# Queues of a fused DeltaNet and mixer kernel, searched anew up to the second token group

## The chip, the cores and the metric

The kernel runs on one core of a Trainium2 chip. The metric is the device time of one execution in microseconds: the median over the runs, 591.4 us here, from 591.33 to 591.42 over three runs. Two versions that differ by less than about 0.2% can hardly be told apart by it.

## The reference

Two blocks follow each other. The first is a delta-rule attention over 4 batches, 8 heads, 768 tokens and a head width of 48, written as a recurrence over tokens:

```python
k_n = k / (np.linalg.norm(k, axis=-1, keepdims=True) + 1e-06)
for t in range(S):
    y[:, :, t] = q_t @ state
    v_old = state^T k_t
    state = state + beta_t * outer(k_t, v_t - v_old)
```

The second mixes its output x (4 x 768 x 384): a low-rank mix over tokens and a channel block.

```python
h = xt @ U @ V                       # rank 32, over the 768 tokens
u = x + h.transpose(0, 2, 1)
ch = np.maximum(u @ w_ch1, 0.0) @ w_ch2      # 384 -> 1536 -> 384
return u + ch
```

The weights U, V, w_ch1 and w_ch2 come as float64 and are turned into float32 on the core.

## The kernel before

**Units.** The attention is cut into 8 units of work, one for each half (384 tokens, six chunks of 64) of each batch; units 0 and 1 make up batch 0. A unit loads k, q and v, turns k and q on PE (L668 or L405, copied out by ACT at L682), forms the k-by-k products (L704; diagonal blocks taken out by ACT at L714 and DVE at L717, the rest copied by ACT at L725, for units 0 and 1 spread by L729) and the q-by-k products (masked by DVE at L736). It norms the keys (`norms`: L611 on ACT, L614 to L619 on DVE, the rows for v at L625 and L628). Then it solves the triangular systems (`blocks`): DVE transposes the diagonals (L781), does fifteen pairs of small multiply and subtract steps (L790, L796), transposes back (L803) and the halves are joined on PE, ACT and DVE (L812 to L926: PE L847, L861, L887/890, L905/908; ACT L852, L895, L914, L926; DVE L865). Two slots of SBUF hold the units in turn, so unit 2 can be loaded when the recurrence is through unit 0.

**Recurrence.** `recur` walks the twelve chunks of a batch: PE L1107, L1135, L972, L986, with DVE at L1120 and L1147 and ACT's L956 that writes the rows of x. For units 0 and 1 `prepare` (PE L1011 and L1022, ACT L1030 and L1035) folds the triangular solution into k and v first.

**Weights.** Fourteen slices are loaded in float64 halves (L1221: slice 0 is U, 1 is V, then six of w_ch1, six of w_ch2) into three buffers in turn, and DVE converts each with five instructions (L1244, L1250, L1256, L1262, L1272), with ACT's L1229 in between. A slice's load waits until its buffer's last slice is through L1262. L1179 forms sums of the second matrix's slices.

**Token groups.** Each batch has three groups of 256 tokens. `front` of a group mixes tokens (PE L1469, DVE L1476, PE L1486, DVE L1495) and turns the result (PE L405 or L1514, ACT L1517). `wide` runs the channel block: PE L1580, ACT L1545, sums on DVE (L1607), PE L1695, and DVE adds the products to X (L1620), which SP writes out.

**Order.** Nothing is scheduled at run time. Every part of the work is a coroutine that yields operations, and for each engine a written list, `ORDER`, says whose operation comes next. An entry is the name of a part: its ordinal, and behind dots that of the parts it started. `11.4` is the fifth part that part 11 started. The function `run` walks the five lists and emits an instruction as soon as it is at the head of its engine's list; the instructions of an engine then run strictly in the list's order, and a list of DMA issues on SP or POOL is such a queue too. Planned costs (`cost`, `lat`, the constants `SPAN, PHASE = 3.413, 2.0` of the array's clock) are used when the lists are searched and to emit in a sensible order; they change no instruction.

The names that the change and the prediction use:

- 0, 1: loads of k, unit 0; 2, 3: beta of the first and second halves (PE L579, ACT L587, DVE L595); 4: the recurrence of batch 0, with 4.0 to 4.3 its `prepare` steps.
- 8: norms of unit 0; 9 and 10: its k and q products; 11: its `blocks`, with 11.2 and 11.4 the joins of the two halves of its chunks and 11.1 and 11.3 the copies of the diagonals; 12 to 17: its loads of q, v and z (two parts each, one on SP and one on POOL; z is a second copy of some of k).
- 18 to 29: the same for unit 1 (18 norms, 19 and 20 products, 21 `blocks`, 22, 23 k; 24, 25 q; 26, 27 v; 28, 29 z). 30 to 37: unit 2 (33 `blocks`; 34 k, 35 q, 36 v, 37 z, a part for both queues each). 38 to 45: unit 3.
- 78: weights: 78.0 to 78.13 load slices 0 to 13, 78.14 to 78.27 convert them, 78.26.1 and 78.27.1 form sums.
- 81, 82, 83: `front` of groups 0, 1, 2 of batch 0; 98, 99, 100: their `wide`.

Of the kernel before, what the change touches and what calls it, by code (L numbers as in the profile page):

```python
# [26 lines left out]
def kernel(  # L27
# [100 lines left out]
    def advance(i, value, at):  # L128
# [28 lines left out]
        5.4 99.1*2 5.5 40.0.0.0 5 83 99.2*2 99.3*2 99.4 48.0 99.4 41.2*2 47.0 99.7 47.1 47.0.0.0 47.1.0.0  # L157
        41.4*2 99.5*2 48.1 41.2 41.4*2 41.2 99.7 99.8 48.1.0.0 5 99.8 5.6 5 48.0.0.0 5 99.9 5 99.9 5.7 5*2
        99.9 5 5.6 99.9 5.8 5.7 5 99.10 5*2 100.0 5.9 5 100.0 5.8 5 100.0 5 100.0 5.9 5 5.10 5 100.1 5.11 5
        5.10 100.1 5 5.11 100.1*2 84 100.2*2 100.3*2 100.4*2 100.5 100.7 100.5 49.2*2 55.0.0.0 84 55.1.0.0  # L160
        100.7 100.8 49.2 49.4*2 49.2 100.8 84 100.9*2 6 85 100.9 6 100.9 56.0.0.0 56.1.0.0 6 100.10 49.4*2
        6.0 6 101.0*2 85 6.1 6 101.1*2 6 101.1 6 101.1 6.2 6 101.2*2 6.1 6 101.2*2 6 6.3 6.2 101.3 6 101.3 6
        6.4 6.3 6 101.4 6 101.4 6.5 6 101.4 6 101.4 6.4 6 6.5 101.5*2 101.7*2 57.2*2 57.4*2 86 57.4*2 57.2*2
# [1613 lines left out]
```

## Time and profile before

| | before |
|---|---|
| median of three runs | 591.4 us |
| lowest, highest | 591.33, 591.42 us |
| the profiled execution | 589.15 us |
| its span, first to last instruction | 587.4 us |
| PE busy | 545.3 us (93%) |
| PE weight loads busy | 491.1 us (84%) |
| DVE busy | 456.2 us (78%) |
| ACT busy | 227.3 us (39%) |
| POOL busy | 118.1 us (20%) |
| granted PE clock, mean | 0.939 |

The profile is one execution. Its time, 589.15 us, is the span and 1.75 us around it, and lies 2.25 us under the median of the runs. Rows give the start from the first instruction, the busy time of a group of equal instructions, the engine, the line of the kernel, and in brackets the idle time of the engine ahead of it with what ended it. "SPq" and "POOLq" are the queues that issue DMAs. PEclk is the share of the full clock that the array was granted. A wait for several semaphores is put down to one of them.

### The profile page before, as it was taken

To read this page: it belongs to the slowest core of one execution; us is meant where nothing else is said; L and a number is where in the kernel's file an instruction comes from. 1 tells how busy PE (TensorE), PEld (TensorE's weight loads), DVE (VectorE), ACT (ScalarE), POOL (GpSimd) and SP (SyncE) were. 2 spreads that over 40 slices of the span, in tenths; PEclk is the share of its full clock that TensorE was granted. 3 is DMA by queue.
4 is the path that set the end of the run, shared out by engine and by line. 5 is a ranking of instruction groups with operands and counts; after the bars stand their busy time and mean duration, and the time that the engine had idled before them with its cause. 6 is when DMAs were issued, how large, how long until landed. Compare 5 with 4: busy or idle time off the path is not lost.

```text
span 587.4 us, 25542 instructions
## 1 busy us (share of the span) xinstructions
PE 545.3 (93%) x11460; PEld 491.1 (84%) x11460; DVE 456.2 (78%) x1086; ACT 227.3 (39%) x483; POOL 118.1 (20%) x205
## 2 busy tenths in 40 slices
PE   5697778799999999999999999999999999999997
PEld 4586677588888987997897798988889999999997
DVE  6898999999899898899878888888547574555552
ACT  4447476544433623344344305324423422131220
POOL 8132050311205304340252253301000000000000
PEclk9576666799999999999999999999999999999999
DMA  9634676652104314223212433200000000000013
GB/s 157 85 76 128 192 188 166 134 91 63 29 4 83 68 22 83 74 53 63 48 30 61 80 75 71 60 29 3 2 5 1 2 1 1 1 2 1 1 42 119
DMA packets 79213, 35.17 MB, mean 60 GB/s; under 512 B 65600, under 2 KB 76992, under 8 KB 79104
## 3 DMA queue, kind: packets, MB, share of 16 engines
q1 hardware_dynamic: 71200, 24.10, 18.9%
q0 software_dynamic: 6304, 9.15, 7.2%
q8 instruction: 90, 1.47, 1.0%
q10 hardware_dynamic: 1600, 0.30, 0.3%
q14 instruction: 19, 0.16, 0.1%
HBM read 28.80 MB, written 4.72 MB: 57 GB/s over the span
## 4 chain that ended last, share of the span: by engine, by line
PE 79%; DVE 7%; ACT 5%; DMA 4%; issue 3%; SPq 1%; POOL 1%; DVEq 0%; ACTq 0%; POOLq 0%
PE P L1695 24%; PE P L1580 12%; PE P L1430 12%; PE P L393 10%; PE P L704 3%; DMA wide<-in_moe_w_ch_dram 2%; PE P L668 2%; PE P L1066 2%; PE P L1090 1%; PE P L972 1%; PE P L1486 1%; PE P L986 1%; PE P L1135 1%; PE P L1514 1%; PE P L861 1%
## 5 line engine op out<-in xcount | busy, mean ns | idle before, releaser
L1695 PE MATMUL P<-w_sb,hs 128*128 128x192 f32 x480 | 84.2, 329 | 0.1
L1580 PE MATMUL P<-ut,w_sb 128*128 128x256 f32 x348 | 81.8, 386 | 0.1
L1695 PEld LDWEIGHTS P<-w_sb,hs 128*128 128x128 f32 x480 | 77.7, 190 | 1.3 <-issue 0.3
L1580 PEld LDWEIGHTS P<-ut,w_sb 128*128 128x128 f32 x348 | 64.1, 190 | 9.4 <-issue 0.6
L796 DVE TENSOR_TENSOR xt<-xt,prod 128x112 f32<-128x112 f32 (+21 forms) x200 | 64.6, 323 | 6.9
L790 DVE TENSOR_TENSOR prod<-gs,xt 128x112 f32<-128x112 f32 (+21 forms) x200 | 63.7, 319 | 3.9
L1620 DVE TENSOR_TENSOR X<-X,P 128x192 f32<-128x192 f32 x86 | 29.6, 349 | 36.1 <-PE P L1695 34.2
L1545 ACT ACTIVATE hs<-P 128x512 f32<-128x512 f32 x42 | 24.8, 597 | 62.1 <-PE P L1580 51.0
L393 PE MATMUL P<-ut,w_sb 64*64 64x256 f32 x624 | 43.0, 384 | 1.2 <-ACT hs L1545 0.9
L956 ACT COPY X<-P 64x192 f32<-64x192 f32 x96 | 30.0, 312 | 28.8 <-PE P L986 27.2
L704 PE MATMUL P<-slot 48*64 48x64 f32 x1536 | 33.5, 245 | 1.9 <-ACT slot L682 1.6
L704 PEld LDWEIGHTS P<-slot 48*64 48x64 f32 x1536 | 30.0, 157 | 6.1 <-ACT slot L682 2.5
L933 POOL MEMSET slot<- 32x384 f32 x32 | 13.4, 420 | 102.6 <-PE P L890 40.4
L1412 DVE TENSOR_TENSOR hs<-hs,P 128x512 f32<-128x512 f32 x30 | 20.1, 684 | 17.5 <-PE P L1430 9.2
L1695 PE MATMUL P<-w_sb,S 128*128 128x192 f32 x192 | 33.7, 330 | 0.0
L926 ACT COPY slot<-zz 32x384 f32<-32x384 f32 x64 | 32.3, 508 | 1.0
L1099 ACT COPY z<-P 128x192 f32<-128x192 f32 x36 | 11.5, 319 | 53.3 <-PE P L1090 46.4
L1695 PEld LDWEIGHTS P<-w_sb,S 128*128 128x128 f32 x192 | 31.1, 190 | 0.6 <-DVE xt L796 0.3
L548 POOL DMA_DIRECT2D slot<-in_k_dram x44 | 28.7, 657 | 12.3 <-PE P L1135 10.6
L668 PE MATMUL P<-ident,slot 128*128 128x128 f32 x108 | 20.0, 343 | 11.3 <-DMA slot<-in_k_dram 5.7
L1430 PE MATMUL P<-slot 128*128 128x128 f32 x240 | 29.7, 276 | 0.0
L1695 PE MATMUL P<-w_sb,slot 128*128 128x192 f32 x168 | 29.1, 327 | 0.0
(171 smaller groups left out, 1140.9 us busy)
## 6 DMA issues: line engine op xcount, KB each, us to landing
out_dram<-X SPq DMA_DIRECT2D x22, 192.0 KB, 2.0
X<-in_moe_w_ch_dram SPq DMA_DIRECT2D x10, 384.0 KB, 4.4
wide<-in_moe_w_ch_dram SPq DMA_DIRECT2D x10, 384.0 KB, 4.4
slot<-in_k_dram SPq DMA_DIRECT2D x48, 72.0 KB, 3.7
slot<-in_k_dram POOLq DMA_DIRECT2D x44, 72.0 KB, 3.1
slot<-in_v_dram SPq DMA_DIRECT2D x32, 72.0 KB, 3.7
slot<-in_v_dram POOLq DMA_DIRECT2D x32, 72.0 KB, 3.2
hs<-in_moe_w_ch_dram SPq DMA_DIRECT2D x4, 384.0 KB, 5.7
```

Source lines behind the costliest of these rows:

```text
L393: nc.tensor.matmul(to[half(g)], w[half(r), half(g)], x[half(r)], start=start, stop=stop, skip_group_check=True,)
L548: queue.dma_start(out=t[half(1 - g if name == "z" else g), :, to, 0:D], in_=src[b, 4 * g + s, hf * UC * L : (hf + 1) * UC * L, :].rearrang ...
L668: nc.tensor.transpose(p_t[:, c // 3, c % 3], t[:, c, 2 * j : 2 * j + 2].rearrange("p s d -> p (s d)"), ident,)
L704: nc.tensor.matmul(p_g[half(g ^ (par * i)), par, c], kq[rows, c, j, 0, half(g)], kq[rows, c, j, i, half(g)], start=True, stop=True,)
L790: nc.vector.tensor_tensor(out=prod, in0=gb[:, :, j : j + 1, j + 1 :].to_broadcast([128, split, m, w]), in1=xb[:, :, 0:m, j : j + 1].to_bro ...
L796: nc.vector.tensor_tensor(out=xb[:, :, 0:m, j + 1 :], in0=xb[:, :, 0:m, j + 1 :], in1=prod, op=ALU.subtract,)
L926: nc.scalar.copy(pg[quarter(i), :, at, :, a : a + BK], cut(zc, h)[quarter(i)].rearrange("p r (c j) t -> p r c j t", j=2),)
L956: nc.scalar.copy(x[half(c % 2), c // 2, 4 * D * g : 4 * D * (g + 1)].rearrange("p (j r d) -> p r j d", r=2, d=D), states(p_y)[half(g)],)
L1430: nc.tensor.matmul(bank[:, q], w_block(w)[:, q // 2, 128 * (q % 2) : 128 * (q % 2) + 128], token(b, i, t), start=c == 0 and q == 0, stop=True,
L1580: nc.tensor.matmul(p_f[:, x], w(x, t), ut[:, t], start=(t == 0), stop=(t == KT - 1))
L1620: nc.vector.tensor_tensor(out=to, in0=to, in1=p, op=ALU.add)
L1695: nc.tensor.matmul(to, of[0], of[1], start=of[2], stop=of[3], skip_group_check=True)
```

## The change

The same steps stand in the same five lists, in another order from the start up to a point in the `wide` of group 0 (98.7 on PE, and the same place on the other engines); from there on the lists are equal but for one entry (79) that issues nothing. No step is added, taken away or computed in another form. One line of the lists is saved, so lines behind L178 move up by one in the changed kernel; this text uses the numbers of the kernel before.

What is moved, engine by engine:

- PE: the beta matmuls of the second half (`3`) before unit 1's second k turn (19.1) and not around its products; the joins 11.2 and 11.4 of unit 0 closer together; the joins of unit 1 (21.2, 21.4) later among the first steps of the recurrence; in `wide` of group 0 the first product (98.0) ahead of group 1's mix (82), and all of 98.2 ahead of unit 2's join 33.2.
- DVE: U's last conversion before unit 0's norms; V's conversion (78.15) earlier; the transpose back of unit 1 (L803) ahead of the two masks 20.1.0.0; two small steps of unit 2 (30, 32.0.0.0) ahead of slice 12's conversion (78.26); the sums 78.26.1 ahead of unit 2's last steps (33).
- ACT: the warm-up of the square root table (`1`) first; the copies of the diagonals and L729 of unit 1 in another order; relu of 98.0 behind the copies for group 1 and unit 3.
- POOL: beta (`2`) ahead of the first loads; loads of q and z in another order.
- SP: three of the four pieces of V (78.1) behind k and q of unit 1, the last one between the v loads of unit 0 (14); v of unit 1 (26) partly ahead of the last of 14; one more load of unit 2 ahead of the second half of slice 9 (78.9); loads of unit 3 in another order.

The lists, cut to the part that differs most:

```diff
     ORDER = dict(
         pe="""
-        9.0 9.1 9.0.0.0 9.1.0.0 2*2 19.0 19.1 3 19.0.0.0 3 19.1.0.0 10.0 10.1 10.0.0.0 20.0 11.4 10.1.0.0
-        11.4 11.2*2 11.4*2 11.2*2 20.1 11.4*4 20.0.0.0 11.2*4 20.1.0.0 4.1 4.0*2 4.1 21.2*2 4 4.4 21.2 4
-        21.2 4.5 4 21.4*2 21.2 4 4.5 4.6 4*2 21.2 4.6 21.2*2 4.7 4*2 4.8 4.7 4 21.4 4.9 4 21.4 4 4.9 4.8
-        4.2*2 21.4*2 4 4.10 21.4*2 4*2 4.10 4.11 4*2 4.11 4.3 32.0 31.0 4.3 31.1 4.12 4 31.0.0.0 31.1.0.0 4
-        4.12 32.1 4.13 4*2 4.13 4.14 4 4.15 4 4.14 4.15 79 32.0.0.0 81 32.1.0.0 81*2 40.0 82 98.0*2 39.0
-        39.1 82 98.1 40.1 39.1.0.0 39.0.0.0 98.1 98.2 33.2*2 98.2 98.3*2 98.4 33.4*2 33.2 98.4 33.2 98.5
-        33.4*2 33.2*2 98.5 98.7 83 33.2 33.4 33.2 33.4 98.7 33.4*2 98.8 5 5.0 5 40.1.0.0 5 98.8 5.1 5 98.9 5
-        98.9 5 5.1 98.9 5 98.9 5.2 5 98.10 5 5.2 5.3 5 99.0 5 99.0 5 5.3 5.4 5 99.0 5 99.0 5.5 5 99.1*2 5
...
+        9.0 9.1 9.0.0.0 9.1.0.0 2*2 19.0 3*2 19.1 19.0.0.0 19.1.0.0 10.0 10.1 10.0.0.0 20.0 11.4*2 11.2*2
+        11.4*2 10.1.0.0 11.2*2 20.1 11.4*4 20.0.0.0 11.2*4 20.1.0.0 4.0 4.1 4.0 4.1 4 21.2*2 4.4 4 21.2*2
+        4.5 21.4 4 21.4 4 21.2*2 4.5 4.6 4*2 4.7 21.2*2 4.6 4*2 4.7 4.8 4 21.4 4.9 4 21.4 4 4.9 4.8 4.2*2
+        21.4*2 4 4.10 4 21.4*2 4 4.11 4.10 4*2 4.3 4.11 32.0 31.0 4.3 31.1 4.12 4 31.0.0.0 31.1.0.0 4 4.12
+        32.1 4.13 4*2 4.13 4.14 4 4.15 4 4.14 4.15 32.0.0.0 79 81 32.1.0.0 81*2 40.0 98.0 82 98.0 39.0 82
+        98.1 39.1 40.1 39.1.0.0 39.0.0.0 98.1 98.2*2 33.2*2 98.3*2 98.4 33.2*2 33.4*2 98.4 98.5 33.2 33.4*2
+        33.2 98.5 98.7 33.2*2 83 33.4*2 98.7 33.4*2 98.8 5 5.0 5 40.1.0.0 5 98.8 5.1 5 98.9 5 98.9 5 5.1
+        98.9 5 98.9 5.2 5 98.10 5 5.2 5.3 5 99.0 5 99.0 5 5.3 5.4 5 99.0 5 99.0 5.5 5 99.1*2 5 5.4 99.1*2
...
         dve="""
-        9.0.0 9.1.0 78.14*3 9.0.0.0*2 9.1.0.0*2 78.14 11 2 8 11*12 8 11 19.0.0.0*2 11*4 19.1.0.0*2 11.4 21
-        78.14 3 10.0.0.0 11.2 18 78.15 21 78.15 10.1.0.0 10.0.0.0 21 18 21 11.4*2 10.1.0.0 11.4 21*3 11.2*3
-        8 21 78.15 21*7 20.0.0.0*2 21*2 20.1.0.0 21 20.1.0.0 78.15*2 21.2 21.4 18 78.16 4 78.16*4 4 78.17*2
-        4 21.2*3 78.17*3 4 78.18*2 4 78.18*3 4 78.19*2 4 78.19 4 78.19 4 78.19 78.20*2 4 78.20 21.4 4
-        78.20*2 21.4 78.21 21.4 78.21*4 4 78.22*2 4 78.22*2 4 78.22 4 78.23*2 4 78.23*3 78.24*5 4 78.25*2
-        31.0.0.0*2 31.1.0.0*2 4 33 4 30 4 78.25 4 33*2 4 78.25*2 33*2 78.26 32.0.0.0 78.26 81 33 78.26 81
-        32.1.0.0*2 78.26 33 78.26 33 82 33*2 32.0.0.0 30 33*8 33.4 33.2 78.26.1*3 39.0.0.0 78.27 98.2.1*3
-        39.1.0.0 78.26.1 39.0.0.0 30 78.27*4 39.1.0.0 33.2*3 33.4*2 78.27.1 33.4 41 98.5.1*2 78.27.1*2
-        98.7.0 98.5.1 78.27.1 38 83 41 98.6 5 98.7.1 41*3 38 98.8.0 5 98.8.1 41*3 5 41 5 41*2 40.1.0.0
...
+        9.0.0 9.1.0 78.14*3 9.0.0.0*2 78.14 9.1.0.0*2 11 2 78.14 8 11*10 8 19.0.0.0*2 11*7 11.4 19.1.0.0*2
+        11.2 21 3 78.15 18 78.15 21*3 10.0.0.0 21 10.0.0.0 11.4 10.1.0.0 21 11.4*2 11.2 21*2 11.2*2 18 78.15
+        10.1.0.0 21 8 21*4 20.0.0.0*2 21*5 20.1.0.0*2 78.15 21.2 78.15 18 78.16*2 4 78.16*3 4 21.4 78.17*2
+        21.2 78.17 4 21.2*2 78.17*2 4 78.18*2 4 78.18*3 4 78.19*2 4 78.19 4 78.19 4 78.19 78.20*2 4 78.20
+        21.4 4 78.20*2 21.4 78.21*2 21.4 78.21*3 4 78.22*2 4 78.22*2 4 78.22 4 78.23*2 4 78.23*3 78.24*5 4
+        78.25*2 31.0.0.0*2 31.1.0.0*2 4 33 4 30 4 78.25 4 33*2 4 78.25*2 33*2 30 32.0.0.0 78.26*2 81 78.26
+        32.1.0.0 81 32.1.0.0 33*5 78.26 82 32.0.0.0 78.26 78.26.1*3 33*8 33.2 30 39.0.0.0 78.27 39.0.0.0
+        78.27 78.26.1 39.1.0.0 33.4 78.27*3 33.2*3 98.2.1 78.27.1*2 33.4*2 39.1.0.0 33.4 41 78.27.1 98.7.0
+        98.2.1 98.5.1*2 78.27.1 98.5.1 98.2.1 38 83 41 98.6 5 98.7.1 41*3 38 98.8.0 5 98.8.1 41*3 5 41 5
...
         act="""
-        1*4 9.0.0 1 9.1.0 9.0.0.0 9.1.0.0 78.14.0 2*2 9.0.0.0*2 8 19.0.0 9.0.0.0 9.1.0.0*3 19.0.0.0 19.1.0
-        19.0.0.0 19.1.0.0 10.0.0 10.1.0 3*2 20.0.0 19.1.0.0 18 11.4.0 11.4 11.4.0 19.0.0.0 19.1.0.0 11.2
-        11.2.0*2 11.4 11.3 11.4 11.1*3 11.4 11.3 11.1 11.3*2 11.2 19.1.0.0 19.0.0.0 20.1.0 78.15.0 11.2*2
-        4.0*2 4.1 21.2 21.2.0*2 78.16.0 4.4 4.1 4.4 78.17.0 21.4.0*2 4.5 21.4 78.18.0 4.5 21.2*2 4.6 78.19.0
-        4.6 21.2 4.7 21.1*2 4.7 21.1*2 78.20.0 4.9*2 4.8*2 78.21.0 4.2*2 21.3 21.4 21.3 21.4 78.22.0 21.3
-        21.4 21.3 78.23.0 4.10 4.11*2 32.0.0 4.10 78.24.0 31.0.0 4.3*2 31.1.0 31.0.0.0 31.1.0.0 4.12*2
-        31.1.0.0 30 31.0.0.0 4.13*2 78.25.0 4.14*2 4.15*2 32.1.0 78.26.0 81 40.0.0 98.0.0 82 39.1.0 39.0.0
-        39.0.0.0 40.1.0 98.1.0 33.2 98.2.0 78.27.0 39.1.0.0 39.0.0.0 33.4 98.3.0 39.1.0.0 33.1*2 98.4.0
-        98.5.0 33.2 33.1*2 33.4 33.2 38 33.2 33.4*2 5 33.3 5.0*2 5 33.3*3 98.9 5.1*2 5*2 99.0 5.2*2 5.3 5
...
+        1*5 9.0.0 9.1.0 9.0.0.0 78.14.0 9.1.0.0 2*2 9.0.0.0 9.1.0.0 8 9.1.0.0*2 9.0.0.0*2 19.0.0 19.0.0.0
+        19.1.0 3*2 19.1.0.0 19.0.0.0 10.0.0 10.1.0 20.0.0 11.4 11.4.0*2 11.2.0 18 19.1.0.0 19.0.0.0 11.2
+        11.2.0 11.4 11.3 11.4 11.1*4 11.4 19.0.0.0 11.3*3 11.2 20.1.0 11.2*2 19.1.0.0*2 78.15.0 4.0*2 21.2.0
+        4.1 21.2.0 4.1 78.16.0 21.2 21.4.0 4.4*2 78.17.0 21.1 21.4 21.4.0 4.5 78.18.0 4.5 21.1 21.2 4.6
+        21.2*2 78.19.0 4.6 21.1 4.7 21.1 4.7 78.20.0 4.9 4.8*2 4.9 78.21.0 4.2*2 21.3 21.4 21.3*2 78.22.0
+        21.4*2 4.10 21.3 78.23.0 4.11*2 4.10 32.0.0 78.24.0 31.0.0 4.3*2 31.1.0 31.0.0.0 31.1.0.0 4.12*2
+        31.1.0.0 30 31.0.0.0 4.13*2 78.25.0 4.14 4.15*2 4.14 32.1.0 81 40.0.0 78.26.0 82 39.0.0 39.1.0
+        39.1.0.0 40.1.0 98.0.0 39.0.0.0 98.1.0 33.2 98.2.0 39.0.0.0 78.27.0 33.4 98.3.0 98.4.0 33.2 98.5.0
+        39.1.0.0 33.2*2 38 33.4 33.1*4 33.4*2 5 33.3 5.0*2 5 33.3*3 98.9 5.1*2 5*2 99.0 5.2*2 5.3 5 5.3
...
         pool="""
-        11.0 13 23 78.0 2*3 17 23 25 23 13 23 25 13*2 25 29 25 21.0 15*2 29 17 15*2 11.3 11.1 11.3 11.1 27*4
-        21.1*2 34*3 35 31.0 35 33.0 21.3*2 35 34 35 43*2 42*4 43 39.0 43 36*2 37 41.0 36 44 36 33.1 37 33.1
-        44*2 33.3 44 33.3 45 51*2 50*4 45 47.0 49.0 51*2 53 41.1*2 52*2 41.3 52*2 53 41.3 110*8 61 55.0 59*6
...
+        2 11.0 2 78.0 2 23*2 13*2 25 23*2 13*2 17 25 21.0 15*2 29 15*2 17 29 25*2 11.3 11.1 27*2 11.1 27
+        11.3 27 21.1*2 34*3 35 31.0 35 21.3*2 35*2 34 33.0 43*3 42*2 36*2 42 36 42 37 39.0 36 43 37 41.0
+        33.1*2 44*2 33.3*2 44*2 45 51*2 50*4 47.0 49.0 51 45 51 53 41.1*2 52*2 41.3 52*2 53 41.3 110*8 61
...
         sp="""
-        0*4 78.1 22*2 12*2 22*2 78.1*2 12 78.1 12 24*3 14*4 24 16 26*4 78.2*2 28 16 78.3*2 78.4*2 28 78.5*2
-        78.6*2 78.7*2 78.8*2 78.9 35 34*4 35*2 78.9 35 78.10*2 78.11*2 36*3 37 36 78.12*2 43*4 37 42*3 45 42
-        44*2 78.13*2 44 45 44 51*4 50*4 52*2 53 52*2 53 110*2 59 110*6 61 59 99.9.1 59*3 61 58*2 59*2
...
+        0*4 22 78.1 22 12 22 24*2 22 16 24*2 12*3 78.1*2 28 14*2 78.1 14 26 14 78.2 16 26*2 78.2 26 78.3*2
+        78.4*2 78.5*2 78.6*2 28 78.7*2 78.8*2 78.9 34 35*2 34*3 35*2 78.9 78.10*2 78.11*2 36*2 37*2 36
+        78.12*2 36 43*4 42*4 44*2 45 78.13*2 44*2 45 51*4 50*4 52*2 53 52*2 53 110*2 59 110*6 61 59 99.9.1
...
```

More of the change, by code (lines that the diff above doesn't have):

```diff
@@ L159 @@
[L159 to L163, printed above, removed]
@@ new lines @@
+        99.9.1 49 99.10.0 5 49 5 49*2 5 49 5 49*2 5 49 5 49*9 46 49*2 84 49 100.2.1*2 49.2 49.4 55.1.0
+        55.0.0 100.5.1*2 100.2.1 100.5.1 100.7.0 84 55.1.0.0 55.0.0.0 55.1.0.0 100.7.1 55.0.0.0 100.6 57
+        100.8.0 54 100.8.1 56.0.0 57*4 56.1.0 6 85 100.9.0 56.0.0.0 56.1.0.0 56.0.0.0 6 57 56.1.0.0 100.9.1
+        100.10.0 57*7 6 57 6 57*2 6 57*2 6 57*3 101.2.1 57 6 57 6 57*2 6 57 6 57*5 6 54 57*3 57.2 101.2.1
+        101.7.0 57.4 101.2.1 101.5.1*3 101.7.1 54 86 101.6 101.8.0 101.8.1 63.0.0 64.0.0 101.9.0 101.9.1
@@ new lines @@
+        63.1.0 63.0.0.0 6 63.0.0.0 101.10.1 101.10.0 64.1.0 63.1.0.0*2 65 62 65*2 6 65 64.0.0.0 62 6
+        64.0.0.0 65*2 6 65*2 6 65*3 6 65 6 102.2.1 65 6 65 6 65*3 6 102.2.1*2 65 6 65 102.5.1*2 65 62 87 65
+        102.5.1 102.7.0 65*3 102.7.1 65 102.8.0 65 102.6 102.8.1 87 65 102.9.0 65 71.0.0 65 102.9.1 102.10.0
+        64.1.0.0*2 71.1.0 65*4 71.1.0.0 65 71.0.0.0 65.4 71.0.0.0 71.1.0.0 65.2 73 72.1.0 72.0.0 70 73*2
+        72.1.0.0 103.2.1 73 72.1.0.0 73*3 103.2.1*2 73 103.7.0 103.5.1*2 72.0.0.0 73 7 103.5.1 103.7.1 73
@@ new lines @@
+        94.1.2 94.2.2 105.1*2 105.3.1 105.3.0 95.0 94.1.3 95.0*4 94.5.0 94.2.3 95.0 105.4.0 94.0 105.2
+        94.4.1 95.0 105.4.1 94.1.4 105.5.0 95.0*2 106.1*2 106.0 91 95.0 106.1 105.6.0 106.0 105.5.1 106.3.0
+        95.1.1 96.0*3 95.2.1 106.0 95.0 95.1.2 95.4.1 106.3.1 106.2 96.0 95.3.1 95.1.3 106.4.0 95.2.2 96.0
+        106.4.1 96.0*3 95.5.0 106.5.0 96.0*2 95.1.4 95.2.3 92 96.1.1 96.2.1 107.0 96.1.2 96.2.2 106.6.0
+        107.1*2 106.5.1 96.2.3 97.0*4 107.1 107.0*2 107.3.0 97.0*2 107.3.1 96.3.1 97.0*3 107.4.0 96.0 96.1.3
@@ L262 @@
+        59*3 61 58*2 59*2 99.10.0 58*2 98.10.0 98.9.1 59 100.9.1 60*4 111*8 67*5 69 100.10.0 67*3 68*3
+        101.10.1 68 112*2 75 112*6 101.9.1 75*2 77*2 75*3 66 75*2 66 102.9.1 74 66 74 69 66 102.10.0 74*2
+        76*4 103.9.1 103.10.0 108.6.0 105.5.1 107.5.1 107.6.0 106.5.1 104.10.1 109.3.1 108.5.1 104.9.1
+        106.6.0 105.6.0 109.5.0 109.5.1 109.6.0
         """,
```

89 lines of the change are left out of this document (37 added, 52 removed).

## The prediction

> **What bounds the kernel now.** I read the page's slices first, then the busy time by stretch, then what the engines wait for.
>
> ```profile
> PE   5697778799999999999999999999999999999997
> DVE  6898999999899898899878888888547574555552
> PEclk9576666799999999999999999999999999999999
> ```
>
> A slice is 587.4/40 = 14.7 us. PE is full and its clock high from the ninth slice on; in the eight slices before, PE has holes, a clock of about a half, and DVE is the full one. The busy time by stretch (columns: length, then busy time and count of PE, PEld, DVE, ACT, POOL; then PE's clock, DMA share, GB/s) says the same in numbers:
>
> ```profile
> 10.00:59.00 49.00, 36.62 (x1126) 33.46 (x1120) 44.10 (x118) 28.59 (x56) 13.92 (x23) 0.65 0.56 106
> 59.00:94.00 35.00, 25.73 (x890) 23.49 (x892) 33.66 (x58) 19.69 (x39) 8.59 (x14) 0.64 0.71 184
> 94.00:118.80 24.80, 20.09 (x592) 16.57 (x588) 23.01 (x48) 14.58 (x27) 6.97 (x12) 0.75 0.67 148
> 155.00:587.40 432.40, 422.58 (x7883) 382.92 (x7881) 316.36 (x772) 144.00 (x326) 71.25 (x121) 1.00 0.17 37
> ```
>
> Up to 118.8 DVE is the bound (44.10 + 33.66 + 23.01 = 100.8 of 108.8 us busy from 10 on); from there PE is (422.58 of 432.40 us behind 155). The switch is the first matmul on finished attention rows: the turn of `front` for group 0, L405, which waits for DVE's L1495. DVE's own waits, in order of time, and that turn:
>
> ```profile
> 10.73 0.26 DVE L1244 TENSOR_SCALAR power<-X 128x192 int32<-128x192 int32 x1 [1.42 <-DMA X<-in_moe_U_dram]
> 24.56 0.74 DVE L717 SCALAR_TENSOR_TENSOR slot<-P,even,slot 128x192 f32<-128x192 f32 x2 [0.23 <-ACT slot L714]
> 52.10 0.56 DVE L736 TENSOR_TENSOR slot<-P,mask_u 128x384 f32<-128x384 f32 x1 [0.94 <-ACT slot L914]
> 93.66 0.56 DVE L1244 TENSOR_SCALAR power<-wide 128x768 int32<-128x768 int32 x1 [0.40 <-DMA wide<-in_moe_w_ch_dram]
> 114.67 0.72 DVE L1244 TENSOR_SCALAR power<-X 128x768 int32<-128x768 int32 x1 [0.64 <-DMA X<-in_moe_w_ch_dram]
> 118.83 0.93 PE L405 MATMUL P<-ident,X 64*64 64x64 f32 x48 [1.31 <-DVE X L1495]
> ```
>
> The steps are the same before and after, and the queues are the same behind group 0's `wide`. So the change is worth (a) what it moves L405, plus (b) what PE waits more or less between L405 and that point. I go through both in order of time.
>
> **Start, to 33 us.** The load of U stays the third transfer on POOL's queue, but two beta transfers (48 KB) stand ahead of it in place of a q and a k piece (72 KB): DVE's 1.42 us wait for it can shrink by 0 to 1.4. The pieces ahead are little smaller, and behind the wait ACT's L714 comes soon; I take 0.3.
>
> ```profile
> 14.91 0.26 DVE L595 STREAM_TRANSPOSE betas<-beta_rows 128x128 f32<-128x128 f32 x1
> 15.30 0.18 DVE L614 TENSOR_SCALAR norm<-norm 128x32 f32<-128x32 f32 x1
> ```
>
> U's last conversion, L1272, moves from behind unit 1's L781 to between L595 and L614, where DVE has 15.30 - 15.17 = 0.13 free: 0.1 gained, and neither less than 0 nor more than that gap. The 0.23 wait on L714 of unit 1 should go, because unit 1's k arrives earlier:
>
> ```profile
> 10.00:15.00 5.00, 3.73 (x128) 3.33 (x122) 4.24 (x10) 3.12 (x7) 3.73 (x6) 0.90 1.17 172
> 20.13 1.51 PE L668 MATMUL P<-ident,slot 128*128 128x128 f32 x6 [4.89 <-issue]
> 26.76 2.82 PE L668 MATMUL P<-ident,slot 128*128 128x128 f32 x12
> 29.18 3.43 SPq L548 DMA_DIRECT2D slot<-in_v_dram  x4
> ```
>
> PE stands for 4.89 us before unit 1's second k turn. No releaser is named; I read it as the last k pieces, since three of the four V pieces (192 KB) are issued ahead of them. After, three V pieces leave the front and about two q pieces (72 KB) enter: 0.43 MB at 172 GB/s is 2.5 us. The batch-1 beta matmuls (L579, `3`) fill part of the gap. So unit 0's q turns (26.76 to 29.58) end near 26.2. DVE does not go faster for that, but L717, now three steps earlier, finds its data. Start: 0.3 + 0.1 + 0.2 = 0.6 gained.
>
> **The 0.94 wait at 52.**
>
> ```profile
> 48.55 1.12 ACT L729 ACTIVATE hs<-slot,even 128x384 f32<-128x384 f32 x2
> 50.26 0.94 ACT L1229 ACTIVATE power<-power,bias_e 128x768 int32<-128x768 int32 x1
> 51.09 0.97 ACT L914 ACTIVATE slot<-P 32x384 f32<-32x384 f32 x2
> 52.57 2.05 DVE L803 STREAM_TRANSPOSE zz<-xt 128x1024 f32<-128x1024 f32 x1
> ```
>
> The changed queue lets L803 (2.05) go ahead of both L736 (`20.1.0.0`), so the PE product that L736 waits for gets two more us. L803 itself must wait for unit 0's last L914, which ends at 52.06. On ACT the two L729 (1.12) and the L1229 (0.94) now stand behind it, so L914 ends near 50.0; DVE is free at 52.10 - 0.94 = 51.16 in the profile, so now at 50.6. The whole 0.94 goes; take 0.9. If L914 didn't move, DVE would wait 52.06 - 50.6 = 1.5 and the change would lose 0.5 here instead: these are the bounds.
>
> **59 to 100 us.** The same work in nearly the same order; the head start of 1.5 is carried, except at one place. SP's second half of weight slice 9 (`78.9`) has eight attention loads ahead of it where it had seven:
>
> ```profile
> 83.88 2.65 SPq L548 DMA_DIRECT2D slot<-in_k_dram  x4
> ```
>
> One is 2.65/4 = 0.66 us, and DVE already waits 0.40 at 93.66 for exactly this slice. Loss between 0 (DVE itself late) and 0.66; I take 0.7 since the wait shows no slack.
>
> **The way to L405.**
>
> ```profile
> 115.32 0.54 DVE L736 TENSOR_TENSOR slot<-P,mask_u 128x384 f32<-128x384 f32 x1
> 115.78 0.54 DVE L1250 TENSOR_SCALAR X<-X 128x768 int32<-128x768 int32 x1
> 116.25 0.34 DVE L1476 COPY tt<-P 128x192 f32<-128x192 f32 x1
> 116.96 0.95 DVE L1256 SCALAR_TENSOR_TENSOR X<-X 128x768 f32<-128x768 uint32 x1
> 117.83 0.95 DVE L1495 TENSOR_TENSOR X<-X,P 128x768 f32<-128x768 f32 x1
> ```
>
> DVE is free at 114.67 - 0.64 = 114.03 and ends L1495 at 118.78: 4.75 us. After, L625 (0.2) and one L736 (0.46, start to start) run in the 0.64 wait for slice 12, then L1244 0.65, L1250 0.47, L1476 0.26, L1256 0.87, the other L736 0.46, L1495 0.95: 4.3 us. One L790/L796 pair moves behind. Gained 0.4; bounds 0 and 0.64.
>
> **Behind L405.**
>
> ```profile
> 129.75 2.86 PE L1580 MATMUL P<-ut,w_sb 128*128 128x256 f32 x12
> 132.54 0.99 PE L847 MATMUL P<-zz,slot 32*32 32x16 f32 x96
> 131.16 1.04 DVE L812 STREAM_TRANSPOSE zz<-zz 128x384 f32<-128x384 f32 x2
> 132.12 2.30 DVE L1179 TENSOR_TENSOR w_sb<-w_sb 128x576 f32<-128x576 f32 x3
> ```
>
> Counted from L405, unit 2's first L847 starts at 132.54 - 118.83 = 13.7. PE now does six more L1580 first (half of 2.86): 15.1. DVE does three L1179 (2.2) ahead of the L812 that L847 needs, and that L812 is now the first of the two: 12.3 + 2.2 + 0.5 = 15.0, and 0.2 for ACT's L1229, which now stands behind two copies. So PE waits 0 to 0.8; I take 0.2.
>
> **Sum:** 0.6 + 0.9 - 0.7 + 0.4 - 0.2 = 1.0 us gained. The profiled execution took 589.15 us (span 587.4), so 588.15 by this sum. The median of the runs is 591.4, 2.25 above the profiled one; taking the same 1.0 off gives 590.4, or 0.17% less. A change under 0.2% (1.2 us) can hardly be told from none.
>
> **Rivals.** *The losses do not come.* Slice 9's wait is covered and L847 finds its data: 0.6 + 0.9 + 0.4 = 1.9 gained, with U at its better bound 2.5: 588.9 to 589.5. For it: the eighth load costs nothing if DVE is itself slowed by the recurrence there. Against: the wait of 0.40 exists.
>
> *V comes too late: slower.* SP's queue now has two v loads of unit 0 ahead of the last V piece, and they wait for unit 0's q turns. DVE's first conversion of V moves to right behind unit 1's L781 and L595, which end at 32.25 in the profile and would end at 31.6 with the 0.6 of the start.
>
> ```profile
> 31.92 0.33 DVE L595 STREAM_TRANSPOSE betas<-beta_rows 128x128 f32<-128x128 f32 x1
> ```
>
> ```profile
> slot<-in_v_dram SPq DMA_DIRECT2D x32, 72.0 KB, 3.7
> ```
>
> In the profile the first v load goes 0.4 before the turns end (29.18 against 29.58); I give two loads 1.3, and take the median of v loads on SP, 3.7 us, for the landing. So V is there 4.6 us (3.7 + 1.3 - 0.4) after the turns: in time if these end by 27.0, and I have 26.2. If they end at 29.58 as before, DVE stands 34.2 - 31.6 = 2.6 us: 591.4 - 1.0 + 2.6 = 593.0. It hangs on my reading of the 4.89 us gap.
>
> *The clock rises late.*
>
> ```profile
> 20.90:24.30 3.40, 3.40 (x74) 2.92 (x73) 3.09 (x12) 0.35 (x1) 0.00 (x0) 0.50 0.57 80
> 27.70:31.10 3.40, 3.40 (x58) 2.95 (x57) 3.40 (x5) 1.80 (x4) 2.14 (x3) 0.50 0.12 25
> 113.00:116.40 3.40, 3.40 (x79) 2.19 (x74) 2.66 (x9) 1.44 (x2) 3.40 (x6) 0.50 1.05 184
> 116.40:119.80 3.40, 2.09 (x98) 1.66 (x93) 3.37 (x8) 0.00 (x0) 2.97 (x6) 1.00 1.36 172
> 104.23 0.88 PE L668 MATMUL P<-ident,slot 128*128 128x128 f32 x6 [0.77 <-ACT X L956]
> ```
>
> Full rate begins at 116.4, 2.4 us before L405. Six L668 take 1.51 at half rate and 0.88 at full, so a PE-bound us at half rate loses 0.42. With L405 at 117.8 and the rise two such stretches later (123.2), 5.4 us lose 2.2: 592.6. It decides from a rise at about 120.2 on.
> The Trainium skill, TensorE: Matmul & The Clock Gate, "What's actually happening", says that one busy window of about 3.4 us releases the clock and that the window runs free of the kernel. By its first half this rival could not be, since PE is busy well ahead of L405; the trace does not agree, with PE 3.40 of 3.40 busy from 20.9 and the clock still 0.50 in 27.7 to 31.1. By its second half the time would change from run to run; the runs lie within 0.09 us, so no run here shows it.
>
> *The head start is lost in the recurrence* (25.73 of 35 us PE busy at a half clock): no change, 591.2.
>
> **How the numbers follow.** Forecast, 589.7 to 591.1: 0.38 (0.15 of it faster by over 0.2%, 0.23 within). Losses absent: 0.28, faster. V late: 0.20, slower. Clock: 0.09, 0.06 of it slower. Recurrence: 0.05, within. Faster 0.43, within 0.31, slower 0.26. The range goes from a little under the second case to a little above V late: 588.4 to 593.4.
>
> **What would show it.** Right: no idle before L736 near 51, L668 of unit 1's second turn by 18, a wait near 1 us for slice 9's L1244, none for slice 12's, L405 near 117.8. Wrong: DVE waiting for `wide<-in_moe_V_dram` near 32, L803 waiting for L914, a clock of 0.50 behind L405, or PE waits of over 0.5 us before L847.

## The result and the profile after

The changed kernel takes 589.38 us (middle of 18 runs, 587.5 to 590.91) against 591.28 us for the kernel before (18 runs, 588.91 to 594.05): a ratio of 0.9965, 95% interval 0.9951 to 0.9979, or 1.9 us less. A second set of 12 runs of the same kernel gave 0.9976 (0.9957 to 0.9995). The profiled execution of the changed kernel took 589.76 us, 0.4 above its middle; that of the kernel before, 589.15 us, lies under 17 of the 18 times of its kernel. So the two profiles, held against each other, show no gain:

```profile
119.67 0.93 PE L404 MATMUL P<-ident,X 64*64 64x64 f32 x48 [1.11 <-DVE X L1494]
```

This is the turn of group 0 (L405 before; lines behind L178 are one lower now). It starts at 119.67, where it started at 118.83. From its start to the end of the span the two executions take the same: 468.6 us before, 468.4 after. The slices of the page:

```profile
PE   5796878789999999999999999999999999999997
DVE  5989998999899898899878888888547574555552
PEclk9956565799999999999999999999999999999999
```

The busy time by stretch (columns as in the prediction):

```profile
10.00:59.00 49.00, 40.35 (x1128) 37.52 (x1128) 43.93 (x118) 27.85 (x56) 14.24 (x23) 0.76 0.53 98
59.00:94.00 35.00, 29.15 (x946) 26.95 (x947) 33.53 (x58) 20.49 (x42) 8.69 (x14) 0.58 0.75 197
94.00:118.80 24.80, 20.22 (x582) 17.00 (x576) 22.63 (x47) 13.28 (x25) 5.49 (x9) 0.70 0.58 138
155.00:588.10 433.10, 423.09 (x7887) 383.20 (x7885) 317.10 (x773) 144.51 (x327) 71.69 (x121) 1.00 0.17 37
```

DVE is still the full engine up to the turn, with nearly the same busy time. Its waits at the start and for slice 9, and the steps where the wait near 52 was:

```profile
10.22 0.56 DVE L678 COPY slot<-P 128x384 f32<-128x384 f32 x1 [2.61 <-PE P L667]
12.36 0.74 DVE L716 SCALAR_TENSOR_TENSOR slot<-P,even,slot 128x192 f32<-128x192 f32 x2 [0.85 <-ACT slot L713]
...
53.18 2.18 DVE L802 STREAM_TRANSPOSE zz<-xt 128x1024 f32<-128x1024 f32 x1
55.28 0.97 DVE L735 TENSOR_TENSOR slot<-P,mask_u 128x384 f32<-128x384 f32 x2
...
95.24 0.56 DVE L1243 TENSOR_SCALAR power<-wide 128x768 int32<-128x768 int32 x1 [2.31 <-DMA wide<-in_moe_w_ch_dram]
```

Two steps of PE that the prediction named, unit 1's second k turn and unit 2's first L847 (L846 now):

```profile
17.16 1.54 PE L667 MATMUL P<-ident,slot 128*128 128x128 f32 x6
...
135.18 0.99 PE L846 MATMUL P<-zz,slot 32*32 32x16 f32 x96
```

The wait of 0.94 near 52 is gone: L802 (L803 before) and behind it L735 (L736) start without one. So is the wait of 0.64 for slice 12. The wait for U is gone too, but DVE waits longer for the second k turn of unit 0 (2.61, where it was 1.49), and at L716 for ACT (0.85, where it did not wait), and the wait for slice 9 has grown from 0.40 to 2.31. Which of these carries the 1.9 us, one pair of profiles cannot say; the experiments cut the change into parts.

### The profile page after: what moved, and what is told of

It reads as the page before. It is cut to its first block, busy times and chain, and to the rows that moved or that the text cites. A ratio compares the mean times of both kernels' runs of the same rounds, so it can differ in the third digit from the quotient of the medians.

```text
span 588.1 us, 25538 instructions
## 1 busy us (share of the span) xinstructions
PE 550.5 (94%) x11460; PEld 497.0 (85%) x11460; DVE 455.9 (78%) x1086; ACT 225.6 (38%) x482; POOL 119.3 (20%) x205
## 4 chain that ended last, share of the span: by engine, by line
PE 81%; DVE 10%; issue 3%; ACT 3%; DMA 2%; SPq 1%; DVEq 0%; ACTq 0%
PE P L1694 24%; PE P L1579 14%; PE P L1429 12%; PE P L392 11%; PE P L703 4%; PE P L667 2%; DVE xt L795 2%; DVE prod L789 2%; PE P L1089 2%; PE P L860 2%; PE P L971 2%; PE P L1065 1%; PE P L1485 1%; PE P L985 1%; PE P L1134 1%
## 5 line engine op out<-in xcount | busy, mean ns | idle before, releaser
L1411 DVE TENSOR_TENSOR hs<-hs,P 128x512 f32<-128x512 f32 x30 | 20.1, 684 | 17.5 <-PE P L1429 9.2
```

## What the runs' spread is made of

One thing in the fourteen profiles of this case changes between executions of the same kernel: when the array runs at full rate. L847 and L704 show it, 72 and 48 equal matmuls each (columns: stretch, length, PE and PEld busy with counts, PEclk, DMA share, GB/s). The kernel before, then `mid_only` (an experiment below), then two stretches of the changed kernel:

```profile
33.50:35.57 2.07, 2.04 (x72) 2.07 (x72) 1.00 0.93 194
```

```profile
34.89:38.61 3.72, 3.72 (x72) 3.72 (x72) 1.00 0.29 63
```

```profile
22.50:23.85 1.35, 1.35 (x48) 1.25 (x48) 1.00 0.01 3
26.75:27.50 0.75, 0.75 (x48) 0.74 (x48) 1.00 0.00 0
```

The same 72 matmuls take 2.07 us in one execution and 3.72 in the other, and the same 48 take 1.35 and, 4 us later, 0.75. All four rows say PEclk 1.00. So the row reads full ahead of the clock's first recorded entry, where nothing is known; the pace of the matmuls is the better witness there. Counting only the stretches that are recorded as full, the array had full rate ahead of L405 for about 36 us in the profile of the kernel before, 25 and 31 us in the two of the changed kernel, and 15 us in that of `mid_only`, which at 595.29 us is the slowest of its 13 runs (middle 590.16) and has L405 at 124.8. Its row of slices reads full where the 72 matmuls went at half pace:

```profile
PEclk9999655789999999999999999999999999999999
```

Its mean clock by the records, 0.957, is the highest of the fourteen profiles, and its time the longest. That the pattern differs between executions of one kernel is shown by the changed kernel's two profiles; that it makes the spread of 3 to 5 us is a reading, but all fourteen bear it out. In the eight profiles with the new middle (a part of the change, below) the full rate ahead of L405 lasts 15 to 31 us and L405 starts at 116.62 to 124.85; in the six without it, 26 to 36 us and 118.83 to 124.09. In both groups L405 is latest where full rate was shortest. A straight line through each group has L405 about 0.4 us earlier for each further us at full rate. What follows from it for the experiments: they are judged by the middle of 12 or more runs (6 and 8 for the kernels on slice 9), and single profiles only where the same wait turns up in several of them.

## The experiments

**Three parts, each alone.** The lists are cut at places where both orders have done the same steps. *Start* is PE up to unit 1's products, DVE up to unit 1's `blocks`, ACT up to unit 1's products, all early loads on POOL and SP. *Middle* is the joins of units 0 and 1 and the first steps of the recurrence, with the two places of the 0.94 wait. *Late* is `front` and `wide` of group 0 and the loads of units 2 and 3. The middle's core:

```diff
         dve="""
-        ... 21*7 20.0.0.0*2 21*2 20.1.0.0 21 20.1.0.0 78.15*2 21.2 21.4 18 78.16 4 78.16*4 4 78.17*2 ...
+        ... 21*5 20.0.0.0*2 21*5 20.1.0.0*2 78.15 21.2 78.15 18 78.16*2 4 78.16*3 4 21.4 78.17*2 ...
         act="""
-        ... 11.3*2 11.2 19.1.0.0 19.0.0.0 20.1.0 78.15.0 11.2*2 4.0*2 4.1 21.2 21.2.0*2 78.16.0 ...
+        ... 11.3*2 11.2 20.1.0 11.2*2 19.1.0.0 19.0.0.0 78.15.0 4.0*2 21.2.0 4.1 21.2.0 4.1 78.16.0 ...
```

Of the start, SP's queue; of the late part, PE's:

```diff
         sp="""
-        0*4 78.1 22*2 12*2 22*2 78.1*2 12 78.1 12 24*3 14*4 24 16 26*4 78.2*2 28 16 ...
+        0*4 22 78.1 22 12 22 24*2 22 16 24*2 12*3 78.1*2 28 14*2 78.1 14 26 14 78.2 16 26*2 78.2 26 ...
         pe="""
-        ... 40.0 82 98.0*2 39.0 39.1 82 98.1 40.1 39.1.0.0 39.0.0.0 98.1 98.2 33.2*2 98.2 98.3*2 ...
+        ... 40.0 98.0 82 98.0 39.0 82 98.1 39.1 40.1 39.1.0.0 39.0.0.0 98.1 98.2*2 33.2*2 98.3*2 ...
```

> The kernel before with only the lists' start changed: PE up to the products of unit 1, DVE up to unit 1's `blocks`, ACT up to unit 1's products, POOL's and SP's first 33 entries (and SP's z load of unit 1). The wait of 0.94 near 52 us and all that lies behind it keep the old order. My sum: 0.6 us gained, 590.7 against 591.3. Rival, from the profile after, in which unit 0's first L781 starts at 14.42 instead of 13.04: the new order of the first transfers brings unit 0's k later, and this part loses 0.5 to 1.4, 591.8 to 592.7; then its first L781 starts near 14.4 again. Second rival: the late k belongs to that one execution, and the first L781 starts near 13.0.

> The kernel before with only the middle changed: L803 of unit 1 ahead of both L736, ACT's L914 of unit 0 ahead of the two L729 and of V's L1229, and the joins of units 0 and 1 and the first steps of the recurrence in the new order (PE entries 36 to 90, DVE 68 to 126, ACT 55 to 108). My sum: the 0.94 wait goes, 0.9 gained, 590.4 against 591.3. Rival: DVE's 0.9 is taken up by a wait further on (weights or recurrence, at a clock of a half), 591.3.

> The kernel before with only the part from `front` of group 0 on changed, and with the loads of units 2 and 3 in the new order (PE from entry 118, DVE from 170, ACT from 124, POOL from 42, SP from 47). My sum: slice 9 comes 0.66 later (loss 0.7 at most, if DVE is there in time), 0.4 gained ahead of L405, 0.2 lost at L847: 0.5 slower, 591.8 against 591.3. Rival (the losses do not come): 0.4 gained, 590.9. If all of the gain of the change were here, 589.4.

> The changed kernel again, for a second profile and a second set of times. The times should give the same 589.4, 0.3 to 0.4% under the kernel before. If the clock's half-rate stretches lie elsewhere than in the first profile (where full rate held to 30.3 us), the stretches come with the execution, not with the order. If unit 0's first L781 starts near 14.4 again, its lateness comes with the order; near 13.0, with the execution.

Measured, with the ratio to the kernel before: start 592.57 us (1.0016, 0.9989 to 1.0042), middle 590.16 (0.9979, 0.9959 to 1.0000), late 593.65 (1.0025, 1.0003 to 1.0047), the whole change again 590.21 (0.9976, 0.9957 to 0.9995). Only the middle is on the gaining side, with the time that was expected (590.4). The start loses as its rival had it, but without the rival's sign: the first L781 of unit 0 starts at 13.28, not near 14.4. The late part loses more than the 0.5 expected, and the whole change gains 0.24% where 0.3 to 0.4% was expected. In the second profile of the changed kernel unit 0's first L781 starts at 13.75; in `mid_only`, with the old start, at 15.00. So the 14.42 that looked like a loss by the order is within what one execution differs from another (old start 13.04 to 15.00 in five profiles, new start 13.28 to 14.42 in nine).

**The PSUM pairs held still.** `run` also decides, while it emits, which of the four PSUM pairs a step writes to, by its planned times. A cut list therefore changes pairs far behind the cut. Two of the parts were run again with the pairs written down. The middle was not; worked out from its kernel, 29 of 306 steps take other pairs than in the kernel before, all inside the middle.

```diff
-    SPAN, PHASE = 3.413, 2.0
+    SPAN, PHASE, PICK = 3.413, 2.0, "0123010231203202012300..."
...
         if x is None:
-            return banks, [(y,) for y in banks]
+            want = int(PICK[state.get("picks", 0)])
+            return banks, [(want,)] if want in banks else []
```

> As start_only, with one thing held still: which of the four PSUM pairs a PE step takes. In start_only the new order of the first steps led to other pairs in 281 of 306 steps to the end of the kernel (in the whole change, 74 of 306, all ahead of 98.8); here the steps from the first join behind unit 1's products on take the pairs of the kernel before. start_only stood at 592.57 against 591.4. My sum for the start: 590.7. If the pairs had carried start_only's loss: 590.3 to 591.3. If the order of the start itself loses: 592.5 again.

> As late_only, with the PSUM pairs held still: ahead of `wide`'s first product those of the kernel before, behind it those of the changed kernel, which are the old ones again from 98.8 on (in late_only 207 of 306 steps took other pairs, to the end). late_only stood at 593.65 against 591.4. My sum: 591.8. If the pairs had carried late_only's loss: 590.9 to 591.3, and no stretch of half rate far behind L405 (late_only's profile has one at 446). If this part of the order loses by itself unless the front half goes with it: 593.6 again, with DVE's wait for slice 9 near 2.

Start 592.72 (1.0015, 1.0001 to 1.0030), late 592.68 (1.0018, 1.0006 to 1.0031). The start's loss is not one of pairs. Of late's, some may be: 1.0025 became 1.0018, which the intervals do not tell apart. Alone, both parts lose about 1 us, with intervals that just leave out no change.

**Two parts together.** Singly they add up to a loss, together they gain; the parts two by two, with the PSUM pairs held still, complete the table.

> Start and middle in the new order, everything from `wide` of group 0 on and the loads of units 2 and 3 in the old one; PSUM pairs held still as in start_kept. Singly the parts gave start +1.1, middle -1.2, late +1.1 us, which add up to +1.0, but the whole change gave -1.1 to -1.9: about 2.5 us lie in parts acting together. If start and middle need each other and the late part only costs: 588.3 to 589.3 against 591.5, faster than the changed kernel. If these two merely add: 591.4.

> Middle and late part in the new order, the start in the old one; PSUM pairs held still. If the two merely add: 591.4 against 591.5. If the late part was searched for the DVE and PE times that the middle gives, and costs only without it: 589.5 to 590.3, about as the changed kernel.

> Start and late part in the new order, the middle in the old one (the changed kernel with the wait of L736 on L914 put back); PSUM pairs held still. If the two merely add: 593.7 against 591.5. If the middle is worth only its own 0.9 to 1.2 on top of the changed kernel's 589.7: 590.6 to 590.9. Its profile should have DVE's wait at L736 again, 0.9 or more.

| new order in | ratio to before | 95% interval |
|---|---|---|
| start | 1.0015 | 1.0001 to 1.0030 |
| late | 1.0018 | 1.0006 to 1.0031 |
| start and late | 1.0017 | 0.9997 to 1.0036 |
| middle | 0.9979 | 0.9959 to 1.0000 |
| start and middle | 0.9985 | 0.9967 to 1.0002 |
| middle and late | 0.9987 | 0.9969 to 1.0004 |
| all three | 0.9965; again 0.9976 | 0.9951 to 0.9979; 0.9957 to 0.9995 |

Every kernel with the new middle lies under 1, every one without it at or over 1.0015. Putting the middle in moves the ratio by 0.0021 (alone), 0.0030 (with start), 0.0031 (with late) and 0.0052 (with both; 0.0041 by the second set): 1.2, 1.8, 1.8 and 3.1 us of 591.4. The start moves it by +0.0015, -0.0001, +0.0006 and -0.0022 in the four settings, late by +0.0018, +0.0002, +0.0008 and -0.0020: about nothing on the mean. The two parts alone lie just outside their intervals; the other differences are no larger than the two intervals behind each of them combined. In the three pairs the expectation that the parts merely add came nearest (591.4, 591.4 and 593.7 expected, 591.19, 591.30 and 593.29 measured); all three together do not add: their ratios would make 1.0012, and the whole has 0.9965 and 0.9976.

One place where this may lie shows in the profiles. From the start of the last conversion of slice 11 (L1272) to the end of group 0's L1495, DVE needs 6.2 to 6.6 us with the middle and the late part both old (three profiles) and 6.0 to 6.9 with both new (six). With only the late part new it needs 6.8 to 7.7 (three), with only the middle new 6.9 and 8.5. In these five mixed ones DVE waits 0.6 to 1.6 us there for PE, in the other nine 0 to 0.3. Two of these waits, in `late_kept` and in `start_mid` (L738 is L736, L1478 is L1476):

```profile
117.35 0.56 DVE L738 TENSOR_TENSOR slot<-P,mask_u 128x384 f32<-128x384 f32 x1 [0.60 <-PE P L706]
```

```profile
117.38 0.36 DVE L1478 COPY tt<-P 128x192 f32<-128x192 f32 x1 [0.87 <-PE P L1471]
```

So the old late part may fit the old middle, and the new one the new. But in most of the mixed profiles the array was also at half rate for longer in this stretch (3.8 to 7.0 us, in the other nine 1.9 to 5.0), and single profiles can't separate the two.

Where the middle acts can be seen. On ACT the last two L914 of unit 0 start 5.5 to 5.6 us behind the one ahead of them in the six profiles without it, and 3.9 to 4.6 us in the eight with it. In the changed kernel they stand ahead of the last two L728 (L729) and of L1228 (L1229), and wait for PE:

```profile
47.90 0.48 ACT L913 ACTIVATE slot<-P 32x384 f32<-32x384 f32 x1
...
51.89 0.99 ACT L913 ACTIVATE slot<-P 32x384 f32<-32x384 f32 x2 [0.28 <-PE P L907]
52.90 1.12 ACT L728 ACTIVATE hs<-slot,even 128x384 f32<-128x384 f32 x2
53.93 0.92 ACT L1228 ACTIVATE power<-power,bias_e 128x768 int32<-128x768 int32 x1
```

Without the middle DVE waits at L736 in all six profiles, from 0.36 to 1.57 us; with it, none of eight has such a wait over 0.3 us. Three of the six, in `start_kept`, `late_kept` (there L738 is L736 and L916 is L914) and `start_late`:

```profile
53.21 0.56 DVE L738 TENSOR_TENSOR slot<-P,mask_u 128x384 f32<-128x384 f32 x1 [1.01 <-ACT slot L916]
```

```profile
53.99 0.56 DVE L738 TENSOR_TENSOR slot<-P,mask_u 128x384 f32<-128x384 f32 x1 [1.57 <-ACT slot L916]
```

```profile
54.25 0.56 DVE L736 TENSOR_TENSOR slot<-P,mask_u 128x384 f32<-128x384 f32 x1 [1.43 <-ACT slot L914]
```

From unit 0's first L781 until L803 and both L736 of unit 1 are done, the six profiles without the middle need 41.0 to 43.7 us (mean 42.2), the eight with it 40.7 to 42.7 (mean 41.5): 0.7 us, less than single profiles of a group differ. So the wait is gone wherever the middle is in, but its price is read from the runs. The middle is a block of many moves, and which of them carries it was not tried further.

**The load of slice 9.** DVE waited 2.31 us for it in the first profile of the changed kernel and 2.65 in the second. In one run the second half of the slice goes back behind seven attention loads, in the other it is the first of all; the PSUM pairs are those of the changed kernel.

```diff
         sp="""
-        ... 78.9 34 35*2 34*3 35*2 78.9 78.10*2 ...
+        ... 78.9 34 35*2 34*3 35 78.9 35 78.10*2 ...
```

```diff
         sp="""
-        ... 78.9 34 35*2 34*3 35*2 78.9 78.10*2 ...
+        ... 78.9*2 34 35*2 34*3 35*2 78.10*2 ...
```

> The changed kernel with one SP entry back in its old place: the second half of weight slice 9 (78.9) behind seven attention loads and not eight. All else, the PSUM pairs too, as in the changed kernel, whose 30 runs have a middle of 589.7. DVE waits 2.31 and 2.65 us for this slice in the two profiles of the changed kernel. If that wait is on the path, it shrinks by one load, 0.66: 589.0. If it is covered: 589.7, with the wait no shorter or another in its place.

> The changed kernel with the second half of slice 9 issued right behind the first, ahead of all eight attention loads; the PSUM pairs as in the changed kernel. If DVE's wait for slice 9 (2.31, 2.65) is on the path and nothing else is late: it goes, 587.2 to 587.6 against 589.7. Rival: the loads of unit 2, each 0.6 later, make PE's first turn of unit 2 (L668, which waits 1.22 and 1.56 at 96 already) later, and DVE stands elsewhere: 588.5 to 589.7.

> sl9_first once more (slice 9's second half ahead of all eight attention loads), since its six runs, 587.44 to 591.17, overlap with those of the changed kernel. If it is better than the changed kernel: 588.3 to 588.9, its interval under 0.9965. If the six runs were lucky ones: 589.7.

One load less ahead shows no gain: 589.8 us, ratio 0.9968 (0.9951 to 0.9984), where the changed kernel has 0.9965 and 0.9976. The eight runs lie 0.2 us above the thirty of the changed kernel on the mean, plus or minus 0.9, so a gain of 0.66 isn't quite ruled out. In the profile slice 9 is not waited for, but DVE itself comes late to it (95.53; in the changed kernel it stood ready at 92.93 and 91.00), behind a wait for PE's recurrence:

```profile
90.75 0.35 DVE L1119 TENSOR_TENSOR z<-slot,P 128x192 f32<-128x192 f32 x1 [1.81 <-PE P L1106]
```

This execution, 591.25 us, is the second slowest of its eight, so it doesn't say what a shorter wait is worth in the others.

With the slice ahead of all eight loads the time falls: 588.5 us (0.9947, 0.9927 to 0.9967), and again 587.98 (0.9935, 0.9911 to 0.9960), six runs each. The twelve have a mean of 588.3, the 30 of the changed kernel 589.8: 1.4 less, plus or minus 0.8. This version beats both kernels, by less than the 2.1 to 2.5 that the removal of the whole wait was expected to give. In its second profile DVE has no wait of over 0.3 us from 40 to 95, where the changed kernel waited for slice 9; the next is for slice 10 (two lines higher here, L1245 for L1243):

```profile
95.51 0.56 DVE L1245 TENSOR_SCALAR power<-X 128x768 int32<-128x768 int32 x1 [0.65 <-DMA X<-in_moe_w_ch_dram]
```

In its first profile DVE waited 1.07 us at 91.84 for PE's recurrence (L1136). The rival's mechanism, that unit 2's loads would then be late for PE, did not happen: unit 2's first k turn starts at 94.57 and 93.31 without a wait for a load, where the changed kernel has 96.59 and 95.00.

## Why the prediction was right, and where it was not

The sign, and the 1.9 us within the range, were right; the likeliest value, 1.0 us gained, was low, and 589.38 lies below the forecast's own 589.7 to 591.1. By its steps:

- **The 0.94 wait: right, and most of the result.** The mechanism is the one named, L803 ahead of L736 and L914 ahead of L729: the wait is gone in all eight profiles with the middle and there in all six without. L914 came about 1.5 us earlier, not the 2.06 that the prediction had, since it then waits for PE's L908; that was enough. The term was 0.9; the block that holds it is worth 1.2 alone and 1.8 to 3.1 with the other parts. That this wait is all that the block is worth is not shown. Without the middle, the wait is longer than the 0.94 of the profile before in three of the five others (1.01, 1.43 and 1.57, but also 0.36 and 0.87). Why all three together are 2 to 3 us better than the sum of the three alone stays open; the waits for PE ahead of L1495 are one candidate. That a head start of the start's is lost again in this wait for L914 would explain some of it, but then start and middle should have been better than their sum by more than the 0.2 us (0.5 by the ratios) that was measured.
- **Start, 0.6: not found.** U's wait did go, but its time went into two other waits. With the old start (here `mid_late`, numbers one higher than before) and with the new one (the changed kernel), the second k turn:

```profile
7.03 1.51 PE L669 MATMUL P<-ident,slot 128*128 128x128 f32 x6 [0.42 <-DMA slot<-in_k_dram]
...
10.76 0.26 DVE L1245 TENSOR_SCALAR power<-X 128x192 int32<-128x192 int32 x1 [1.62 <-DMA X<-in_moe_U_dram]
```

```profile
8.67 1.51 PE L667 MATMUL P<-ident,slot 128*128 128x128 f32 x6 [1.65 <-DMA slot<-in_k_dram]
```

  The prediction priced the transfers ahead of U on POOL's queue and not what the new order does to unit 0's own k pieces. These are issued at the same places on the queues of SP and ACT in both orders, with the betas now beside them from 2.8 us on. The two k pieces that SP issues last take a median of 4.7 us from issue to landing in the changed kernel, 3.9 in the kernel before. PE waits 1.0 to 1.7 us for this turn's k in the nine profiles with the new start. In the five with the old one it waits 0.42, 0.52, 0.53, 1.28 and 1.77, and DVE then waits for U the less: 1.62, 1.56, 1.42, 0.67 and not at all. So the two waits trade places within the old order too. Whether the betas bring the longer one no run tells, since none moves them alone. DVE's first L781 comes no earlier. Unit 1's second k turn by 18 was right (17.16).
- **Slice 9's eighth load, -0.7: not found.** Seven or eight loads ahead make no difference that the runs show (589.8 and 589.7). The wait is real, and not near 1 us as forecast but 2.31 and 2.65: DVE stands ready for the slice at 92.93 and 91.00, where it did at 93.26 before, so that a head start ends in this wait. Only the place ahead of all eight loads gains, 1.4 us.
- **The way to L405, +0.4, and L847, -0.2: the first found in the profiles, the second not.** The wait for slice 12 is gone: from where DVE was free for it to the end of L1495 (L1494) the two profiles of the changed kernel take 4.1 and 4.4 us, where the prediction had 4.3 and the profile before 4.75. L846 starts at 135.18 without a wait, so the second loss did not come. In the times the late part as a whole is worth about nothing on the mean, and loses 1 us alone. L405 itself is at 119.67 and 118.06 in the two profiles, not near 117.8.
- **The rivals.** The result is that of "the losses do not come" (588.9 to 589.5), though not by its terms: the start's gain was not there, and the middle's was larger. Its better bound, 2.5, doesn't follow from the prediction either: with U's wait of 1.4 all gained, the three gains make 3.0. V too late did not happen: V's first conversion starts at 33.64 with no wait, and the q turns ended at 26.7, near the 26.2 that I had. Of the way from 29.58 to 26.2 the prediction prices 2.5 us, which gives 27.1; the other 0.9 it only names.
- **The clock.** I wrote that the runs lie within 0.09 us, so that no run shows the free-running window. Eighteen runs lie within 5.1 us: three runs were too few to say so. The Trainium skill, TensorE: Matmul & The Clock Gate, "What's actually happening", which has the window free-running and the same kernel varying from run to run, agrees with the profiles here, and the variation is larger than the change. In the two profiles of the changed kernel the first recorded fall of the clock is at 30.3 and at 15.3 us. The same holds for the sum: it was set against a profile 2.1 us under the middle of its runs.

## What to carry to other kernels

Before pricing terms of half a microsecond from one profile, find out how far single executions lie apart, and compare a cut of the change by many runs of each part. The parts of a changed order need not add up: try them alone, in pairs and together, and hold still what the planner decides on the side (here the PSUM pairs). In this kernel a load that DVE waited for gained 1.4 us by going ahead of the whole group it shares a queue with; one place in that queue showed no gain.

## What the runs showed of the hardware

The clock can fall far behind the start, where PE is otherwise full. In the profile of `late_only`, the slowest of its runs, one stretch at half rate follows one in which PE was busy for 1.75 of 3.40 us (columns as in the prediction):

```profile
442.70:446.10 3.40, 1.75 (x33) 1.54 (x27) 3.33 (x9) 1.55 (x6) 0.00 (x0) 1.00 0.00 0
446.10:449.50 3.40, 3.40 (x18) 3.40 (x17) 0.00 (x0) 1.76 (x3) 0.00 (x0) 0.50 0.00 0
```

From the start of L405 to the end this execution takes 471.7 us, the others of this case 467.5 to 469.9. It was seen once, so what it hangs on is open. Open is also what brings the clock up: in the row of `mid_only` shown above PE is busy for 3.72 of 3.72 us, and the 96 L861 behind it still take 55 ns each, where 48 of them take 33 in the kernel before. First `mid_only`, then the kernel before:

```profile
38.70 5.28 PE L861 MATMUL P<-zz,S 64*64 64x16 f32 x96
```

```profile
35.61 1.56 PE L861 MATMUL P<-zz,S 64*64 64x16 f32 x48
```
